# A list-scheduled attention + MoE kernel: one q/k load per head, a first head in halves, warm-up transposes, and a scheduler that leaves spare time behind DMAs

## The chip, the cores and the metric

The kernel runs on one NeuronCore of a Trainium2 chip. TensorE (PE in the profile; its weight loads are PEld) does the matrix products, VectorE (DVE), ScalarE (ACT) and GpSimd (POOL) do the elementwise work, and SyncE (SP) issues the DMAs. Each engine works through its own list of instructions in order; semaphores tie the lists together. The metric is the device time of one launch in microseconds (us): the median of three runs of the kernel before is 790.98 us (788.99 to 792.19).

## The reference

Inputs are float32. Attention has 2 batches, 8 heads, 768 positions and head size 64; a query sees only keys whose 6-bit hash (the signs of a projection) equals its own. Two MLP stages follow on 1536 tokens.

```python
q_bits = (np.einsum('bhsd,dk->bhsk', q, proj) > 0)      # k_bits likewise, 6 bits -> bucket
mask = q_bucket[:, :, :, None] == k_bucket[:, :, None, :]
scores = np.where(mask, scale * np.matmul(q, k.transpose(0, 1, 3, 2)), -1e9)
attn = softmax(scores)                                   # denominator + 1e-9
x = np.matmul(attn, v)            # -> [1536, 512]
g = s * relu(x @ w_in)**2 + b     # w_in [512, 2048]
x = g @ w_out                     # w_out [2048, 512]
h = ((x @ w1) * (x @ w2)) @ w3    # w1, w2 [512, 1024], w3 [1024, 1024]
out = h @ moe2_w_out              # [1024, 512]
```

## The kernel before

Precision comes from splitting: a float32 operand is written as a high and a low float32r part, and one product becomes three matmuls (high·high, low·high, high·low).

**Attention.** There are 16 heads (`heads`), each cut into 3 units of 256 queries (`units`), 48 in all. `load(n)` brings q and k of a head, transposed, into one tile `t` of 128 partitions (q in the lower 64, k in the upper 64) with two DMAs, and v into `tv`. `prep(n)` splits `t` into q1 (high part, `split_h`) and k2 (low part, `split_l`), has TensorE project them on `proj` (`bits`, two halves of 384 columns), turns the signs into plus and minus values (`mask`, VectorE) and moves 64-partition pieces into the four operand tiles q1, q2, k1, k2 (`move`: kh_lo, kh_up, qh, ql, mq, mk). For the first head the moves are copies of 768 columns on ScalarE, VectorE or GpSimd; for the others they are DMAs between on-chip tiles. v is split likewise into `vv` (`vh`, `vl`). `unit(m)` then runs, per 128 queries, the score product (`sc`, 4 matmuls), its row maximum (`negm`), two small factors (`gate`, `bias`) and the exponential on ScalarE (`p`); then the transposes of p (`t`), their split (`pt`) and the product with v (`o`).

**MLP.** `layer1` runs the first MLP for each batch: 32 weight pieces `raw_...` of 512 KB are loaded and converted in six steps (`convert`, `piece`; conv0 to conv5, the first on VectorE, the last on GpSimd or VectorE), saved to DRAM for the second batch (`save_`) and loaded again (`again`). Its products are `h` and `x` (twelve matmuls for a tile), summed into `acc`. `layer2` first folds w3 and the last weight matrix into one (`fold`, tile `psw`: eight steps j of four tiles, for two halves), then computes `a`, `b`, their product `ab` and the output `y`.

**What sets the order.** Nothing is written in its final order. Every operation is handed to `Plan.op` with its engine, an assumed duration, a rank, what it reads and writes, and other engines it may run on instead. `Plan.emit` works out a due time for each operation from the ends backwards (factor table `SLACK`, offsets `AT`), adds a fixed offset by name (`SHIFT`) and then plays a list schedule: whichever engine is free takes the ready operation of lowest rank, with a penalty for waiting (`LOSS`), and an operation is held ready at `free + TAIL + LATE + LAG_TO` after its producer. `LATE` is an extra delay of some DMAs, by name. The tables hold numbers from a search. All loads and DMA moves are issued by SP, in the order of the list.

```python
end = free[e] + self.TAIL[e] + self.late(o)
...
x["ready"][f] = max(x["ready"][f], free[e] if e == f == "pe" else early + self.LAG_TO[f])
```

Of the kernel before, what the change touches and what calls it, by code (L numbers as in the profile page):

```python
# [1033 lines left out]
```

## Time and profile before

| | us |
|---|---|
| median of 3 runs (lowest, highest) | 790.98 (788.99, 792.19) |
| the profiled execution | 791.12 |
| its span, first to last instruction | 789.0 |
| TensorE busy | 756.0 (96%) |
| VectorE busy | 509.1 (65%) |
| ScalarE busy | 404.3 (51%) |
| GpSimd busy | 333.4 (42%) |

Times are counted from the first instruction of the span. TensorE's busy share is near the whole, so the time is its work plus the time it stands idle. TensorE runs at one of two clocks, 1.2 or 2.4 GHz; a granted clock of 1.00 in the windows is the higher, 0.50 the lower one. A wait is put down to the engine and line that ended last before it.

### The profile page before, as it was taken

How to read it: one execution, taken by the hardware profiler on the slowest of the kernel's cores; microseconds unless marked ns; L12 is line 12 of the kernel's file. 1: busy time of each engine (PE TensorE's matmuls, PEld its weight loads, DVE VectorE, ACT ScalarE, POOL GpSimd, SP SyncE). 2: the span in 40 equal slices, each digit the busy share in tenths (PEclk: the TensorE clock that was granted, in tenths of full speed). 3: DMA queues.
4: the chain of work that ended last, by engine and by line, in shares of the span. 5: the costliest groups of instructions: out<-in, count | busy, mean ns of one | idle time of the engine just before them, and what ended most of it. 6: DMA issues, size and time to landing. Idle time of an engine off the chain costs nothing.

```text
span 789.0 us, 12252 instructions
## 1 busy us (share of the span) xinstructions
PE 756.0 (96%) x4464; PEld 712.3 (90%) x4464; DVE 509.1 (65%) x1008; ACT 404.3 (51%) x769; POOL 333.4 (42%) x358
## 2 busy tenths in 40 slices
PE   5999989899999999999999999999999999999997
PEld 4888878799999998999998999889999999999995
DVE  4899998999999989888767664756786010110110
ACT  4888889676576677577453522533554111111111
POOL 2676877674565475554322232223336021121221
PEclk9999999999999999999999999999999999999999
DMA  7445465666575764763348788554421000001001
GB/s 213 121 104 139 104 171 142 189 183 182 182 215 153 228 169 148 218 216 108 107 160 288 257 289 312 187 199 145 166 104 54 1 1 9 32 1 41 1 27 53
DMA packets 36172, 110.83 MB, mean 140 GB/s; under 512 B 5136, under 2 KB 7312, under 8 KB 36112
## 3 DMA queue, kind: packets, MB, share of 16 engines
q1 hardware_dynamic: 36112, 110.06, 45.2%
q8 instruction: 35, 0.57, 0.3%
q14 instruction: 25, 0.20, 0.1%
HBM read 68.22 MB, written 24.12 MB: 117 GB/s over the span
## 4 chain that ended last, share of the span: by engine, by line
PE 70%; DVE 13%; DMA 5%; ACT 5%; issue 3%; POOL 2%; SPq 0%; ACTq 0%; POOLq 0%; DVEq 0%
PE x L721 14%; PE h L721 11%; PE b L721 8%; PE a L721 8%; PE y L972 8%; PE sc L493 5%; PE t L540 5%; DVE negm L503 3%; PE psw L933 3%; PE o L546 3%; PE o L547 3%; DVE pt L582 2%; DMA raw_wo<-in_wo 2%; ACT p L526 2%; DMA raw_w<-in_w3T 2%
## 5 line engine op out<-in xcount | busy, mean ns | idle before, releaser
L721 PE MATMUL x<-g,w_wo 128*128 128x384 f32 x768 | 152.9, 342 | 1.3 <-DVE pt L582 0.7
L721 PE MATMUL h<-x,w_wi 128*128 128x384 f32 x768 | 152.1, 341 | 1.9 <-DVE acc L815 1.7
L721 PEld LDWEIGHTS x<-g,w_wo 128*128 128x128 f32 x768 | 133.4, 189 | 4.7 <-DVE pt L582 1.4
L721 PEld LDWEIGHTS h<-x,w_wi 128*128 128x128 f32 x768 | 132.9, 189 | 4.4 <-DVE acc L815 2.1
L526 ACT ACTIVATE p<-sc,bias,gate 128x768 f32<-128x768 f32 x96 | 95.7, 997 | 30.0 <-DVE bias L518 16.5
L957 DVE SCALAR_TENSOR_TENSOR ab<-b,ab 128x384 f32<-128x384 f32 x32 | 17.8, 558 | 123.9 <-ACT ab L954 123.9
L503 DVE TENSOR_REDUCE negm<-sc 128x1 f32<-128x768 f32 x96 | 90.9, 950 | 9.2 <-PE sc L493 8.4
L963 POOL TENSOR_TENSOR abt<-ab,abt 128x384 fp32r<-128x384 f32 x32 | 33.9, 1061 | 141.5 <-ACT abt L960 141.5
L540 PE MATMUL t<-ident,p 128*128 128x128 f32 x576 | 85.9, 277 | 6.2 <-ACT p L526 2.0
L493 PE MATMUL sc<-k,q 128*128 128x384 f32 x384 | 87.5, 351 | 3.3 <-ACT p L526 2.4
L540 PEld LDWEIGHTS t<-ident,p 128*128 128x128 f32 x576 | 68.6, 142 | 15.2 <-ACT p L526 3.7
L546 PE MATMUL o<-pt,vv 128*128 128x256 f32 x288 | 75.5, 294 | 4.3 <-DVE xf L599 2.8
L336 POOL TENSOR_TENSOR w_w<-raw_w,w_w 128x512 fp32r<-128x512 f32 x31 | 41.7, 1350 | 78.0 <-ACT w_w L334 77.8
L547 PE MATMUL o<-pt,vv 128*128 128x256 f32 x288 | 72.0, 282 | 0.0
L493 PEld LDWEIGHTS sc<-k,q 128*128 128x128 f32 x384 | 66.0, 193 | 6.3 <-ACT p L526 4.0
L721 PE MATMUL a<-x,w_w 128*128 128x384 f32 x384 | 71.1, 334 | 0.0
L721 PE MATMUL b<-x,w_w 128*128 128x384 f32 x384 | 69.7, 335 | 0.0
L582 DVE TENSOR_TENSOR pt<-t,pt 128x512 fp32r<-128x512 f32 x96 | 64.5, 684 | 7.7 <-ACT pt L578 7.2
L721 PEld LDWEIGHTS a<-x,w_w 128*128 128x128 f32 x384 | 67.1, 188 | 0.9
L972 PE MATMUL y<-whl,abt 128*128 128x512 f32 x288 | 67.7, 391 | 0.0
L960 ACT CAST abt<-ab 128x384 fp32r<-128x384 f32 x32 | 16.5, 515 | 99.2 <-PE y L972 96.9
L572 POOL TENSOR_TENSOR pt<-pf,pt 128x512 fp32r<-128x512 f32 x48 | 64.9, 1352 | 5.6 <-ACT pt L568 2.4
(100 smaller groups left out, 1287.4 us busy)
## 6 DMA issues: line engine op xcount, KB each, us to landing
kept_wo<-w_wo SPq DMA_DIRECT2D x24, 512.0 KB, 6.2
w_wo<-kept_wo SPq DMA_DIRECT2D x24, 512.0 KB, 6.0
raw_wi<-in_w_in SPq DMA_DIRECT2D x16, 512.0 KB, 5.2
kept_wi<-w_wi SPq DMA_DIRECT2D x16, 512.0 KB, 3.6
raw_wo<-in_w_out SPq DMA_DIRECT2D x16, 512.0 KB, 5.0
raw_w<-in_w SPq DMA_DIRECT2D x16, 512.0 KB, 3.7
w_wi<-kept_wi SPq DMA_DIRECT2D x16, 512.0 KB, 5.7
raw_w<-in_w3T SPq DMA_DIRECT2D x16, 512.0 KB, 4.4
```

Source lines behind the costliest of these rows:

```text
L336: lambda: nc.gpsimd.tensor_tensor(hl()[:, 1], w, r32(hl()[:, 0]), ALU.subtract),
L493: nc.tensor.matmul(sc()[:, i, :HALF], x[:, t], y[:, i * HALF : (i + 1) * HALF], start=st, stop=not st)
L503: lambda j=j, sc=sc: nc.vector.tensor_reduce(negm()[:, j : j + 1], sc()[:, :, :HALF], AX.XY, ALU.max, negate=True),
L526: lambda j=j, k=k, sc=sc: nc.scalar.activation(ps[j](), sc()[:, :, :HALF], AF.Exp, bias=bias()[:, j : j + 1], scale=gate()[:, j : j + 1], ...
L540: nc.tensor.transpose(tp()[:, e, j * P : (j + 1) * P], flat[:, c * P : (c + 1) * P], ident)
L546: nc.tensor.matmul(o()[:, :U], w, pt()[:, 0, e], start=(c == 0), stop=False)
L547: nc.tensor.matmul(o()[:, :U], w, pt()[:, 1, e], start=False, stop=(c == NC - 1))
L572: lambda pf=pf, pt=pt: nc.gpsimd.tensor_tensor(pt()[:, 1], pf(), r32(pt()[:, 0]), ALU.subtract),
L582: lambda tp=tp, pt=pt: nc.vector.tensor_tensor(pt()[:, 1], tp(), r32(pt()[:, 0]), ALU.subtract),
L721: nc.tensor.matmul(ps()[:, :n], x, y, start=(i == 0 and e == 0), stop=(i == len(terms) - 1 and e == 2))
L963: lambda: nc.gpsimd.tensor_tensor(abt()[:, 1], ab()[:, :TG], r32(abt()[:, 0]), ALU.subtract),
L972: nc.tensor.matmul(y(), abt()[:, p, c], wt()[:, q], start=(i == 0 and e == 0), stop=(i == DF2 // P - 1 and e == 2))
```

## The change

- q and k of a head lie in one input array `qkT`, and a head's tile `t` is one DMA of 128 partitions; the first head's is two, one for each half of the columns.
- The first head's preparation moves to a function of its own, `begin`: every copy is cut in two halves of 384 columns and may run on ScalarE, VectorE or GpSimd; the low part is a subtraction on VectorE; each half waits only for its own half. The first unit's scores wait for the first half of the query operands alone.
- 24 transposes of the identity matrix into an otherwise unused PSUM tile (`warm_up`) stand first on TensorE.
- The scheduler has a table `SPARE`: what a DMA of those names produces counts as ready on the four engines 0.4 to 1.5 us later than before.
- `SLACK`, `AT`, `SHIFT`, `HOLD`, `AHEAD` and `LOSS` hold new numbers, so the order changes in the whole program.

```diff
-SLACK = dict(dma=0.3391, pe=0.5535, dve=0.5716, act=0.4427, pool=0.4279)
+SLACK = dict(dma=0.3487, pe=0.5375, dve=0.5494, act=0.3954, pool=0.4112)
...
-    AHEAD, LOSS = dict(dma=1.714, pe=0.058, dve=0.072, act=0.268, pool=0.156), 39.709
+    AHEAD, LOSS = dict(dma=1.718, pe=0.064, dve=0.089, act=0.249, pool=0.143), 48.706
...
+    SPARE = dict(raw_=1.5, again_=1.5, load_=1.5, kh_=0.5, ql=0.5, qh=0.5, mk=0.4, mq=0.4)
...
+                spare = self.spare(o)
...
-                        x["ready"][f] = max(x["ready"][f], free[e] if e == f == "pe" else early + self.LAG_TO[f])
+                        x["ready"][f] = max(x["ready"][f], free[e] if e == f == "pe" else early + self.LAG_TO[f] + (spare if f != "dma" else 0.0))
...
+        def warm_up():
+            for _ in range(24):
+                nc.tensor.transpose(tw()[:, :P], ident, ident)
+
+        plan.op("warm", "pe", 2.6, -1000, warm_up, [], [(tw, 0)])
...
-            def both():
-                nc.sync.dma_start(t()[0:64], qT[b, h])
-                nc.sync.dma_start(t()[64:128], kT[b, h])
-
-            plan.op(f"load_qk{ph}", "dma", 1.3, LATER, both, (), [(t, 0)])
+            if n == 0:
+                for i in range(2):
+                    c = halves[i]
+                    plan.op(
+                        "load_qk_0", "dma", 0.65, i - 900, lambda c=c: nc.sync.dma_start(t()[:, c], qkT[b, h, :, c]), (), [(t, i)]
+                    )
+            else:
+                plan.op(f"load_qk{ph}", "dma", 0.9, LATER, lambda: nc.sync.dma_start(t(), qkT[b, h]), (), [(t, 0)])
...
+            def ways(key, out, in_, reads, writes):
+                plan.op(
+                    key, "act", 0.4, -500, lambda: nc.scalar.copy(out(), in_()), reads, writes,
+                    (
+                        ("dve", 0.27, lambda: nc.vector.tensor_copy(out(), in_())),
+                        ("pool", 0.42, lambda: nc.gpsimd.tensor_scalar(out(), in_(), 1.0, 1.0, ALU.mult, ALU.mult)),
+                    ),
+                )
...
+            for i in range(2):
+                c = halves[i]
+                last = lambda x, p: [(x, p, 0)] if i else []
+                ways(f"split_h_0{i}", lambda c=c: q1()[:, c], lambda c=c: t()[:, c], [(t, i)], [(q1, 0, i)])
+                plan.op(
+                    f"split_l_0{i}", "dve", 0.47, -500,
+                    lambda c=c: nc.vector.tensor_tensor(k2()[:, c], t()[:, c], r32(q1()[:, c]), ALU.subtract),
+                    [(t, i), (q1, 0, i)], [(k2, 0, i)],
+                )
+                mask(n, i, mm, [(q1, 0, i), (k2, 0, i)])
...
+            if m == 0:
+                need = [(k1, 0), (k1, 1), (k2, 1), (q1, 1, 0), (q2, 0, 0), (q2, 1, 0)]
```

How the instructions stand at three places, before and after. The first is the start of the DMA list on SP and of GpSimd's list: `t` is a head's q and k, `raw_wi` the first MLP's weights, `tv` a head's v, `k_1` the second head's low part. SP before:

```order
L359 DMA pj<-in_projp 128x128
L387 DMA t_169<-in_qT 64x768
L388 DMA t_169<-in_kT 64x768
L387 DMA t_172<-in_qT 64x768
L388 DMA t_172<-in_kT 64x768
L372 DMA s_bc<-in_sv 128x1
L679 DMA raw_wi_0_0_179<-in_w_in 128x1024
L679 DMA raw_wi_0_1_183<-in_w_in 128x1024
L679 DMA raw_wi_0_2_192<-in_w_in 128x1024
```

The same start of SP's list now:

```order
L375 DMA pj<-in_projp 128x128
L416 DMA t_194<-in_qkT 128x384 x2
L743 DMA raw_wi_0_0_197<-in_w_in 128x1024
L743 DMA raw_wi_0_1_199<-in_w_in 128x1024
L743 DMA raw_wi_0_2_201<-in_w_in 128x1024
L419 DMA t_210<-in_qkT 128x768
L420 DMA tv_219<-in_vl 128x384
```

Head 1's load (t_172 before, t_210 now) stood ahead of the three weight loads and stands behind them; its two DMAs are one. GpSimd's first pieces of work after the identity matrix, before:

```order
L418 TENSOR_TENSOR k_0_187<-t_169,q_0_181 128x768
L418 TENSOR_TENSOR k_1_203<-t_172,q_1_194 128x768
L412 TENSOR_SCALAR vv_261<-tv_240 128x6x64
L418 TENSOR_TENSOR vv_261<-tv_240,vv_261 128x6x64
L566 TENSOR_SCALAR pt_1_317<-pf_1_281 128x512
```

GpSimd's first pieces now (q_0 and k_0 are the first head's operands):

```order
L489 TENSOR_SCALAR q_0_213<-q_0_206 64x384 x2
L489 TENSOR_SCALAR q_0_206<-k_0_217 64x384
L441 TENSOR_SCALAR vv_261<-tv_219 128x6x64
L447 TENSOR_TENSOR k_1_263<-t_210,q_1_250 128x768
L630 TENSOR_SCALAR pt_1_336<-pf_1_304 128x512
L636 TENSOR_TENSOR pt_1_336<-pf_1_304,pt_1_336 128x512
```

Both low parts stood ahead of head 0's v (`vv`). Now the copy of v, whose load is issued behind head 1's, stands ahead of head 1's low part `k_1_263`, and the first head's low part has gone to VectorE. On ScalarE head 1's high part still stands ahead of the first exponential.

The second place is VectorE's list where the second batch starts its first MLP (`acc` is the sum that frees a PSUM tile of TensorE, `raw_wo` a weight piece of the last matrix, whose first step is L326, now L342). VectorE before:

```order
L326 TENSOR_SCALAR raw_wo_0_1_1_5734<-raw_wo_0_1_1_5734 128x512
L327 SCALAR_TENSOR_TENSOR raw_wo_0_1_1_5734<-raw_wo_0_1_1_5734 128x512
L333 SCALAR_TENSOR_TENSOR raw_wo_0_1_1_5734<-raw_wo_0_1_1_5734 128x512
L815 COPY acc_5831<-x_3_0_5786 128x384
L326 TENSOR_SCALAR raw_wo_0_2_0_5791<-raw_wo_0_2_0_5791 128x512
L815 COPY acc_5831<-x_3_1_5793 128x384
L327 SCALAR_TENSOR_TENSOR raw_wo_0_2_0_5791<-raw_wo_0_2_0_5791 128x512
L333 SCALAR_TENSOR_TENSOR raw_wo_0_2_0_5791<-raw_wo_0_2_0_5791 128x512
L815 COPY acc_5831<-x_3_2_5802 128x384
```

VectorE at the same place now:

```order
L342 TENSOR_SCALAR raw_wo_0_1_1_5782<-raw_wo_0_1_1_5782 128x512
L879 COPY acc_5836<-x_3_0_5787 128x384
L349 SCALAR_TENSOR_TENSOR raw_wo_0_1_0_5752<-raw_wo_0_1_0_5752 128x512
L879 COPY acc_5836<-x_3_1_5808 128x384
L343 SCALAR_TENSOR_TENSOR raw_wo_0_1_1_5782<-raw_wo_0_1_1_5782 128x512
L349 SCALAR_TENSOR_TENSOR raw_wo_0_1_1_5782<-raw_wo_0_1_1_5782 128x512
L879 COPY acc_5836<-x_3_2_5816 128x384
L879 COPY acc_5836<-x_3_3_5853 128x384
L861 SCALAR_TENSOR_TENSOR rl_2_0_5883<-h_2_0_5842,sw,rl_2_0_5883 128x384
L870 SCALAR_TENSOR_TENSOR g_2_0_5903<-rl_2_0_5883,b_bc,g_2_0_5903 128x384
L342 TENSOR_SCALAR raw_wo_0_2_0_5871<-raw_wo_0_2_0_5871 128x512
```

The first step on piece 0_2_0 stood between the copies of x_3_0 and x_3_1; it now stands behind all four copies, and behind two more operations. Of piece 0_1_1 all three steps stood ahead of the copy of x_3_0; now only the first does, and the others follow the copy of x_3_1.

The third place is TensorE's list at the last steps of the fold (`psw`; w_w_1_4 to w_w_1_7 are converted pieces of w3, `x` the first MLP's second product). TensorE before:

```order
L933 MATMUL psw_0_6480<-w_wo_1_3_0_6404,w_w_1_6_6724 128x512 x3
L933 MATMUL psw_1_6486<-w_wo_1_3_0_6404,w_w_1_6_6724 128x512 x3
L933 MATMUL psw_2_6490<-w_wo_1_3_0_6404,w_w_1_6_6724 128x512 x3
L933 MATMUL psw_3_6495<-w_wo_1_3_0_6404,w_w_1_6_6724 128x512 x3
L721 MATMUL x_3_1_6762<-g_3_0_6528,w_wo_2_0_6252 128x384 x3
L721 MATMUL x_3_1_6762<-g_3_1_6550,w_wo_2_1_6292 128x384 x3
L721 MATMUL x_3_0_6736<-g_3_2_6690,w_wo_2_2_6301 128x384 x3
L721 MATMUL x_2_3_6683<-g_2_3_6521,w_wo_2_3_6333 128x384 x3
L933 MATMUL psw_0_6480<-w_wo_1_3_1_6429,w_w_1_7_6760 128x512 x3
```

TensorE at the fold's steps 4 to 6 now:

```order
L997 MATMUL psw_0_6766<-w_wo_1_2_0_6341,w_w_1_4_6742 128x512 x3
L997 MATMUL psw_1_6777<-w_wo_1_2_0_6341,w_w_1_4_6742 128x512 x3
L997 MATMUL psw_2_6580<-w_wo_1_2_0_6341,w_w_1_4_6742 128x512 x3
L997 MATMUL psw_3_6791<-w_wo_1_2_0_6341,w_w_1_4_6742 128x512 x3
L997 MATMUL psw_0_6766<-w_wo_1_2_1_6378,w_w_1_5_6815 128x512 x3
L997 MATMUL psw_1_6777<-w_wo_1_2_1_6378,w_w_1_5_6815 128x512 x3
L997 MATMUL psw_2_6580<-w_wo_1_2_1_6378,w_w_1_5_6815 128x512 x3
L997 MATMUL psw_3_6791<-w_wo_1_2_1_6378,w_w_1_5_6815 128x512 x3
L997 MATMUL psw_0_6766<-w_wo_1_3_0_6418,w_w_1_6_6842 128x512 x3
L997 MATMUL psw_1_6777<-w_wo_1_3_0_6418,w_w_1_6_6842 128x512 x3
L997 MATMUL psw_2_6580<-w_wo_1_3_0_6418,w_w_1_6_6842 128x512 x3
L997 MATMUL psw_3_6791<-w_wo_1_3_0_6418,w_w_1_6_6842 128x512 x3
```

A step of 12 fold matmuls was followed by 12 of `x` before the next step; now 72 fold matmuls stand in a row, of which the last 36 are shown, and the last step's 12 come three matmuls later.

Further counts over the whole lists: the last conversion step (conv5) stands 3 times on VectorE before and 23 times after, with as many fewer on GpSimd; SP issues 17 loads of q and k instead of 32; ScalarE has 4 fewer casts of whole heads, GpSimd 3 more.

## Rows read from the trace of the kernel before

**Rows 1.** The page: busy time by engine, and the chain of waits by engine.

```profile
PE 756.0 (96%) x4464; PEld 712.3 (90%) x4464; DVE 509.1 (65%) x1008; ACT 404.3 (51%) x769; POOL 333.4 (42%) x358
...
PE 70%; DVE 13%; DMA 5%; ACT 5%; issue 3%; POOL 2%; SPq 0%; ACTq 0%; POOLq 0%; DVEq 0%
```

**Rows 2.** Windows by stage: width, then busy (instructions) of PE, PEld, DVE, ACT, POOL, clock, DMA.

```profile
0.00:24.00 24.00, 13.14 (x47) 11.16 (x48) 11.91 (x34) 12.52 (x20) 7.71 (x12) 0.93 0.71 199
...
40.00:175.00 135.00, 124.48 (x861) 114.44 (x860) 126.49 (x278) 109.38 (x217) 97.84 (x119) 1.00 0.55 144
...
424.00:450.00 26.00, 24.07 (x128) 23.38 (x127) 15.02 (x27) 8.86 (x16) 6.61 (x6) 0.93 0.90 316
...
450.00:600.00 150.00, 148.48 (x785) 138.45 (x784) 101.65 (x169) 64.91 (x113) 50.03 (x42) 1.00 0.55 191
...
782.00:789.00 7.00, 1.92 (x9) 1.26 (x7) 0.69 (x1) 1.17 (x2) 0.00 (x0) 1.00 0.29 112
```

**Rows 3.** Timeline of the first 18 us: start, duration, engine, line, work [idle before <-releaser].

```profile
1.77 0.58 SPq L388 DMA_DIRECT2D t<-in_kT  x1
...
4.30 1.38 SPq L679 DMA_DIRECT2D raw_wi<-in_w_in  x3
...
5.30 0.83 ACT L411 CAST q<-t 128x768 fp32r<-128x768 f32 x1 [3.08 <-DMA t<-in_kT]
...
8.78 1.82 POOL L418 TENSOR_TENSOR k<-t,q 128x768 fp32r<-128x768 f32 x1 [0.76 <-ACT q L411]
...
11.14 2.77 PE L493 MATMUL sc<-k,q 128*128 128x384 f32 x8
...
12.66 0.96 DVE L503 TENSOR_REDUCE negm<-sc 128x1 f32<-128x768 f32 x1 [0.54 <-PE sc L493]
...
15.76 0.99 ACT L526 ACTIVATE p<-sc,bias,gate 128x768 f32<-128x768 f32 x1 [4.46 <-DVE gate L511]
...
16.90 0.97 PE L493 MATMUL sc<-k,q 128*128 128x384 f32 x4 [2.16 <-ACT p L526]
```

**Rows 4.** The tile raw_wi in the first 40 us: the three weight loads' landing.

```profile
DMA to landing us min/median/max: 5.4/6.4/8.3
```

**Rows 5.** Windows of the head, columns as in rows 2.

```profile
0.00:4.00 4.00, 0.00 (x0) 0.00 (x0) 1.03 (x12) 1.49 (x2) 0.69 (x6) 1.00 0.43 116
...
8.00:12.00 4.00, 3.63 (x10) 3.13 (x11) 2.90 (x5) 2.36 (x3) 1.85 (x2) 1.00 0.96 343
...
15.00:17.00 2.00, 0.10 (x1) 0.10 (x1) 0.94 (x4) 1.24 (x3) 0.00 (x0) 1.00 0.83 187
...
18.00:21.00 3.00, 3.00 (x13) 2.90 (x14) 2.15 (x4) 1.61 (x3) 2.57 (x4) 0.50 0.60 137
```

**Rows 6.** Timeline: eight transposes in that last window.

```profile
19.85 1.73 PE L540 MATMUL t<-ident,p 128*128 128x128 f32 x8
```

**Rows 7.** Timeline around 432 us, VectorE and TensorE.

```profile
432.53 0.43 DVE L326 TENSOR_SCALAR raw_wo<-raw_wo 128x512 int32<-128x512 uint32 x1 [2.28 <-DMA raw_wo<-in_wo]
...
433.47 0.79 PE L721 MATMUL h<-x,w_wi 128*128 128x384 f32 x3 [1.74 <-DVE acc L815]
```

**Rows 8.** A window behind it, columns as in rows 2.

```profile
434.00:438.00 4.00, 4.00 (x16) 4.00 (x15) 1.31 (x4) 1.33 (x2) 1.30 (x1) 0.57 0.92 338
```

**Rows 9.** Chain of waits, order of time: start, duration, work (the last four folds).

```profile
526.02 2.80 PE psw L933 x11
...
541.71 2.76 PE psw L933 x12
```

**Rows 10.** Groups by line and shape: busy us, mean ns | idle before, releasers.

```profile
L336 POOL TENSOR_TENSOR w_w<-raw_w,w_w 128x512 fp32r<-128x512 f32 x31 | 41.7, 1350 | 78.0 <-ACT w_w L334 77.8
...
L412 POOL TENSOR_SCALAR vv<-tv 128x384 fp32r<-128x384 f32 x5 | 2.6, 517 | 8.0 <-DMA tv<-in_vl 7.7 <-PE o L547 0.3
...
L337 DVE TENSOR_TENSOR w_w<-raw_w,w_w 128x512 fp32r<-128x512 f32 x1 | 0.7, 696 | 0.0
...
L420 DVE TENSOR_TENSOR vv<-tv,vv 128x384 fp32r<-128x384 f32 x3 | 1.9, 632 | 0.7 <-ACT vv L411 0.7
```

More of the change, by code (lines that the diff above doesn't have):

```diff
@@ L182, in late, with spare @@
         return next((v for k, v in self.LATE.items() if o["engine"] == "dma" and o["key"].startswith(k)), 0.0)
+    def spare(self, o):
+        return next((v for k, v in self.SPARE.items() if o["engine"] == "dma" and o["key"].startswith(k)), 0.0)
     def early(self, o):
@@ L368, in lsh_attention_moe @@
         )
+        tw = plan.tile(ps_t, 3, [P, 512], F32, "t", "warm")
+        def warm_up():
+            for _ in range(24):
+                nc.tensor.transpose(tw()[:, :P], ident, ident)
+        plan.op("warm", "pe", 2.6, -1000, warm_up, [], [(tw, 0)])
         for x, t, src in (("s", s_bc, sv), ("b", b_bc, bv)):
@@ L378, in phase @@
             return "s" if n == 0 else heads[n][0]
+        halves = [slice(i * HALF, (i + 1) * HALF) for i in range(2)]
         def load(n):
@@ L440, in prep @@
-            copy(f"split_h{ph}", (0.73, 0.8), q1, t, [(t, 0)], [(q1, 0)])
-            rest(f"split_l{ph}", 1.8, k2, t, q1, [(t, 0), (q1, 0)], [(k2, 0)])
-            mm = plan.tile(raw_p, 1, [P, S], F32R, "mm", f"mm_{n}")
-            for i in range(2):
-                mask(n, i, mm)
-            bits = [(mm, 0), (mm, 1)]
-            move(f"kh_lo{ph}", k1, lo, q1, up, [(q1, 0)], [(k1, 0)])
-            move(f"kh_up{ph}", k1, up, q1, up, [(q1, 0)], [(k1, 1)])
-            move(f"qh{ph}", q2, up, q1, lo, [(q1, 0)], [(q2, 0)])
@@ L449, in prep @@
-            move(f"ql{ph}", q1, up, k2, lo, [(k2, 0), (k1, 0), (k1, 1), ("bits", n, 0), ("bits", n, 1)], [(q1, 1)])
-            move(f"mq{ph}", q2, lo, mm, lo, bits, [(q2, 1)])
-            move(f"mk{ph}", k2, lo, mm, up, bits + [(q1, 1)], [(k2, 1)])
+                plan.op(key, "dma", 0.65, LATER, lambda: nc.sync.dma_start(r32(out()[a]), r32(in_()[z])), reads, writes)
+            if first:
+                begin(n)
+            else:
+                copy(f"split_h{ph}", (0.73, 0.8), q1, t, [(t, 0)], [(q1, 0)])
+                rest(f"split_l{ph}", 1.8, k2, t, q1, [(t, 0), (q1, 0)], [(k2, 0)])
+                mm = plan.tile(raw_p, 1, [P, S], F32R, "mm", f"mm_{n}")
+                for i in range(2):
+                    mask(n, i, mm)
+                bits = [(mm, 0), (mm, 1)]
+                move(f"kh_lo{ph}", k1, lo, q1, up, [(q1, 0)], [(k1, 0)])
+                move(f"kh_up{ph}", k1, up, q1, up, [(q1, 0)], [(k1, 1)])
+                move(f"qh{ph}", q2, up, q1, lo, [(q1, 0)], [(q2, 0)])
+                move(f"ql{ph}", q1, up, k2, lo, [(k2, 0), (k1, 0), (k1, 1), ("bits", n, 0), ("bits", n, 1)], [(q1, 1)])
+                move(f"mq{ph}", q2, lo, mm, lo, bits, [(q2, 1)])
+                move(f"mk{ph}", k2, lo, mm, up, bits + [(q1, 1)], [(k2, 1)])
@@ L457, in prep, with begin, move, mask @@
             )
-        def mask(n, i, mm):
+        def begin(n):
+            t, _ = raws[n]
+            q1, q2, k1, k2, _ = ops[n]
+            lo, up = slice(0, 64), slice(64, 128)
+            mm = plan.tile(raw_p, 1, [P, S], F32R, "mm", f"mm_{n}")
+            def ways(key, out, in_, reads, writes):
[6 more added lines that the diff above has]
+                )
+            def move(key, i, x, a, y, z, reads, writes):
+                c = halves[i]
+                ways(f"{key}_0{i}", lambda: x()[a, c], lambda: r32(y()[z, c]), reads, writes)
+            for i in range(2):
+                c = halves[i]
+                last = lambda x, p: [(x, p, 0)] if i else []
[6 more added lines that the diff above has]
+                mask(n, i, mm, [(q1, 0, i), (k2, 0, i)])
+                move("kh_lo", i, k1, lo, q1, up, [(q1, 0, i)] + last(k1, 0), [(k1, 0, i)] + ([(k1, 0), (q1, 0), (k2, 0)] if i else []))
+                move("kh_up", i, k1, up, q1, up, [(q1, 0, i)] + last(k1, 1), [(k1, 1, i)] + ([(k1, 1)] if i else []))
+                move("qh", i, q2, up, q1, lo, [(q1, 0, i)], [(q2, 0, i)] + ([(q2, 0)] if i else []))
+                move(
+                    "ql", i, q1, up, k2, lo, [(k2, 0, i), (k1, 0, i), (k1, 1, i), ("bits", n, i)],
+                    [(q1, 1, i)] + ([(q1, 1)] if i else []),
+                )
+                move("mq", i, q2, lo, mm, lo, [(mm, i)], [(q2, 1, i)] + ([(q2, 1)] if i else []))
+                move("mk", i, k2, lo, mm, up, [(mm, i), (q1, 1, i)] + last(k2, 1), [(k2, 1, i)] + ([(k2, 1)] if i else []))
+        def mask(n, i, mm, need=None):
             q1, _, _, k2, _ = ops[n]
```

35 lines of the change are left out of this document (10 added, 25 removed), and 132 rows, old and new, of tables (AT, SHIFT).

## The prediction

> **What bounds the kernel now.** I read the page first. TensorE is busy 756.0 us [rows 1] of a span of 789.0 us, so 33.0 us of idle time is all that an order can win, apart from time at the lower clock. Then the windows by stage [rows 2] say where those 33 us lie: 10.9 us in the first 24 us, 10.5 us from 40 to 175 us, 1.9 us from 424 to 450, 1.5 us from 450 to 600, 5.1 us in the last 7 us; the remaining 3.1 us are spread over the other stretches. From 40 to 175 us VectorE is busy 126.5 of 135 us, so there TensorE waits on VectorE's work, which this change hardly touches. The end is a copy and a DMA, which stay. Two places are left in which the edits can act: the head, and the dip at 432 us.
>
> In the head I read the timeline [rows 3]. The load of k is issued at 1.77 us and ScalarE's split starts at 5.30 us. GpSimd's low part follows, then projections, masks and moves, and the first row maximum stands at 12.66 us. The first exponential starts at 15.76 us and the third group of scores, which has to wait for it, at 16.90 us. From 15 to 17 us TensorE does 0.1 us of work, and the window 18 to 21 us then shows the granted clock at 0.50, the 1.2 GHz level [rows 5]: 1.5 us of full-speed work is lost in it.
>
> At 432 us the timeline [rows 7] shows one in-order stop. VectorE's first step on a weight piece waits 2.28 us for its DMA. The copy of `acc` that frees a PSUM tile stands behind it, and TensorE's next `h` has waited 1.74 us when it starts at 433.47 us. In the 4 us from 434 on the granted clock is 0.57 on the mean [rows 8], which loses 4 x 0.43 = 1.72 us. So this stop costs 1.74 + 1.72 = 3.46 us.
>
> **The change part by part.** The profiled execution took 791.12 us, 2.12 us more than its span and 0.14 us above the median of 790.98 us; I sum against 791.12 us and take the sum as the forecast of the median.
>
> First head in halves. It has the same bytes in the same two issues, so I let the second half land when k does now, about 5.2 us. ScalarE and VectorE cast the halves by then or 0.4 us later. VectorE subtracts each half; the nearest row is the 128x384 subtraction at 632 ns [rows 10], so both low parts are there at about 6.9 us, where GpSimd's whole one starts when the cast ends, at 6.13 us, and takes 1.82 us, to 8.0 us [rows 3]. Two masks and two half moves follow, all on VectorE; at about 0.5 us each, somewhat less than that subtraction, the second operand is there at 8.8 us and the first row maximum can start near 9.3 us instead of 12.66 us: 3.4 us earlier (2.5 to 4 by the unknown casts). From the first maximum to the first exponential 3.1 us pass now [rows 3], with a mask of the second head and a gap among them; I take 2.2 us without these, so the exponential could start at 11.5 us.
>
> The second head, however, loses its place. Its load stood ahead of the three 512 KB weight loads and now stands behind them. On ScalarE its cast stands ahead of the first exponential, and on TensorE its projection stands ahead of the third group of scores. Behind the cast on ScalarE wait both first exponentials, and behind the projection wait all later scores and transposes. When does it land? The last weight load is issued at 5.3 us and lands 8.3 us later, the longest of the three, at 13.6 us [rows 3, 4]. Now the three are issued 1.9 us earlier, since three small issues no longer stand ahead, so the last would land at 11.7 us, and 393 KB more at the 343 GB/s of 8 to 12 us [rows 5] take 1.15 us: 12.85 us. By bytes alone it could be 9.7 us: 2.42 MB stand ahead or are its own, 0.46 MB are moved by 4 us at 116 GB/s [rows 5], and 1.96 MB at 343 GB/s take 5.7 us. If the weights land no earlier than now, it is 14.8 us. I take 12.5 us, near the end that rests on a landing, not on bytes.
>
> From there: head 0's v lands 0.57 us later (197 KB at 343 GB/s), GpSimd casts it in 0.52 us [rows 10], makes the low part in 1.82 us [rows 3], and one projection matmul at the pitch that eight scores show (2.77 us for 8, [rows 3]) takes 0.33 us: 3.24 us in all. The third group of scores so starts at 15.74 us instead of 16.90 us. **Head: 1.2 us gained**; with 9.7 us it is 4.0 us gained, with 14.8 us 1.1 us lost. The 3.4 us that the halves win are thus mostly waited away behind the weights. Everything after is bound by VectorE or TensorE, both of which start earlier by the same amount, so I carry it to the end undiminished.
>
> Warm-up. The 24 transposes start within the first 2 us on an engine that has nothing to do before the first cast ends at 6.13 us. Eight transposes at the lower clock take 1.73 us [rows 6], so 24 end by 7.2 us at the latest, up to 1.0 us after the first half's operands are there. The wait for the second head hides that; without this cover it costs 1.0 us. They lift the clock for the first scores only: after those TensorE waits for the second head from about 10 to 15.7 us. The rows show that after 2 us with hardly any work, from 15 to 17 us, the clock fell to 0.50 [rows 5]. I therefore leave the 1.5 us of clock loss in the sum. The Trainium skill's page TensorE: Matmul & The Clock Gate (HAM oscillation — how this bites in real kernels) says the same against this edit: a long gap on TensorE throws the clock back, whatever was warmed before. By that rule the sum keeps the 1.5 us; were the clock to hold, it would lose them. The trace agrees with the rule at 17 us and at 434 us.
>
> One load for q and k. SP issues 15 loads fewer, of about 0.6 us each, but SP's queue has 0% of the chain of waits [rows 1]; the cover is that later heads are loaded long before their use. Worth nothing; without that cover 0.6 us a head. The Trainium skill's page DMA: Bandwidth & Descriptors (Rules for kernel authors) says that transfers to disjoint halves of the partitions serialize and one of 128 partitions should be used. By it each pair would shorten a little; the rows of the head show 343 GB/s without it, so I add nothing.
>
> Spare time and new ranks. At the 432 us stop the changed order puts the first step on the next piece behind all four copies of `acc`, so that exact stop goes. What is late next there is piece 0_1_1, whose first step stands ahead of the copy of x_3_0. It is issued when VectorE's new last step on piece 0_0_1 has freed its buffer, and some nine operations of about 0.6 us and three `x` tiles lie between, so it is nearly landed when asked for. **3.46 us gained**, between 0 (a like stop in its place) and 3.46.
>
> Conversions on VectorE: 20 more last steps at 696 ns are 13.9 us, where GpSimd needs 1350 ns [rows 10]. Most are after 424 us, where VectorE is busy 117 of 176 us [rows 2]; that slack hides them. Exposed, each would cost at most its 0.7 us. Elsewhere the counts of work between equal score groups differ by a few operations, so I put 0 for the 40 to 175 us stretch, with 2 us either way.
>
> Sum: 791.12 - 1.2 - 3.46 = 786.5 us.
>
> **The rivals.**
>
> The stop comes back. If piece 0_1_1 or another load is some 2 us late with the copies behind it, as at 432 us, the 3.46 us are paid again and only the head is won: 791.12 - 1.2 = 789.9 us. For it: SP holds the same pieces in nearly the same sequence. Against: the first step stands behind more copies.
>
> Slower: folds in a row. TensorE has 72 fold matmuls in a row, where other products lay between. In the trace the last four steps start 15.69 us / 3 = 5.23 us apart, one takes 2.76 us [rows 9]. If the pieces of w3 are converted only at the old pace when TensorE reaches step 4, it waits 2.47 us at each of three steps, 7.4 us: 791.12 - 1.2 - 3.46 + 7.4 = 793.9 us, slower than before. It decides as soon as three pieces come more than 2.76 us apart and the lead of the 36 matmuls ahead is used up. For it: VectorE converts pieces 1_5 to 1_7 just there. Against: those last steps are faster on VectorE, and 36 matmuls are 8.3 us of lead.
>
> Faster than I think: the second head lands at 9.7 us, by bytes, and the gap on TensorE is short enough that the clock holds: 791.12 - 4.0 - 1.5 - 3.46 = 782.2 us. For it: 96% DMA share from 8 to 12 us, so loads really stream. Against: the 8.3 us landing, far behind the bytes.
>
> **How the numbers follow.** The forecast has 0.45, the stop's return 0.25, the folds 0.17, the fast head 0.13. The forecast's own range is 784.0 to 789.0 us (the 40 to 175 us stretch, and the landing). For 8 in 10 I take 781.5 to 793.5 us: it holds the fast head nearly and half of the folds' case. What can be told from no change is 0.5%, 3.95 us: faster is below 787.0 us, slower above 794.9 us. Faster: 0.27 of the forecast's case, all 0.13 of the fast head, 0.02 of the rest, 0.42. Slower: 0.08 of the folds and 0.04 of mishaps beyond the cases, 0.12. The same: 0.46.
>
> **What would show it.** The first row maximum near 9.3 us and the first exponential only after the second head's cast, near 13.3 us, show the halves and the lost place. The third group of scores near 15.7 us shows the head's gain; at 13 us the landing was early, after 16.9 us the head has lost. A window at 0.50 clock between 14 and 20 us shows that the warm-up did not last. No clock window below 1.00 between 420 and 450 us, and no wait of `h` on `acc` above 1 us, show the stop gone. Waits of `psw` of more than 1 us in a row of folds would show the slower rival. I am wrong if the idle time of the 40 to 175 us stretch moves by more than 2 us, since I have put it at nothing.

## The result and the profile after

The changed kernel takes 783.16 us (median of 4 runs, 782.39 to 784.66); the kernel before takes 790.05 us in runs on the same chip (4 runs, 788.99 to 792.19). The ratio is 0.9906, 95% interval 0.9878 to 0.9935. The forecast of 786.5 us had the direction and the two places; the gain is 6.9 us where it had 4.6. The time lies 0.8 us below the forecast's own range of 784.0 to 789.0 us and inside the wider one of 781.5 to 793.5 us. The profiled execution took 784.66 us, 6.46 us less than that of before; its span is 6.1 us shorter.

The page of the kernel after, the two lines that answer to [rows 1]:

```profile
PE 757.7 (97%) x4488; PEld 712.8 (91%) x4488; DVE 522.8 (67%) x1031; ACT 402.8 (51%) x772; POOL 312.9 (40%) x340
...
PE 72%; DVE 18%; ACT 4%; DMA 3%; issue 1%; POOL 1%; SPq 0%; ACTq 0%; POOLq 0%; DVEq 0%
```

VectorE does 13.7 us more and DMA fell from 5% to 3% of the chain. The windows by stage, which answer to [rows 2] (width; busy time and instructions of PE, PEld, DVE, ACT, POOL; clock, DMA share, GB/s):

```profile
0.00:24.00 24.00, 18.29 (x90) 16.02 (x91) 16.88 (x42) 13.60 (x26) 8.41 (x15) 0.86 0.67 199
...
40.00:175.00 135.00, 125.34 (x862) 114.76 (x861) 127.64 (x279) 109.58 (x219) 94.97 (x117) 1.00 0.53 147
...
424.00:450.00 26.00, 26.00 (x152) 25.95 (x151) 18.42 (x34) 11.32 (x21) 4.77 (x4) 1.00 0.80 272
450.00:600.00 150.00, 149.50 (x794) 140.02 (x793) 106.27 (x181) 64.98 (x112) 32.18 (x25) 1.00 0.57 200
...
776.00:783.00 7.00, 1.71 (x8) 1.09 (x6) 0.69 (x1) 1.17 (x2) 0.00 (x0) 0.79 0.29 112
```

From 424 to 450 us TensorE neither waits nor slows down; before it was idle for 26 - 24.07 = 1.93 us there and lost 0.07 x 26 = 1.82 us at the lower clock. From 450 to 600 us its idle time fell from 1.52 to 0.50 us. The last 7 us are nearly as they were: 5.3 us idle where it was 5.1. For the first 24 us the timeline says more; these rows answer to [rows 3] and [rows 7] (start, duration, engine, line, work [idle before <-releaser]):

```profile
3.84 0.51 ACT L486 CAST q<-t 128x384 fp32r<-128x384 f32 x1 [1.63 <-DMA t<-in_qkT]
...
9.04 1.15 PE L553 MATMUL sc<-k,q 128*128 128x384 f32 x5 [0.67 <-DVE k L488]
...
9.52 1.82 DVE L567 TENSOR_REDUCE negm<-sc 128x1 f32<-128x768 f32 x2 [0.54 <-PE sc L553]
...
11.45 0.83 ACT L440 CAST q<-t 128x768 fp32r<-128x768 f32 x1 [2.38 <-DMA t<-in_qkT]
...
12.53 0.99 ACT L590 ACTIVATE p<-sc,bias,gate 128x768 f32<-128x768 f32 x1 [0.25 <-DVE gate L575]
...
14.93 1.48 PE L553 MATMUL sc<-k,q 128*128 128x384 f32 x4
...
428.34 0.43 DVE L342 TENSOR_SCALAR raw_wo<-raw_wo 128x512 int32<-128x512 uint32 x1 [0.52 <-DMA raw_wo<-in_wo]
429.11 0.56 DVE L879 COPY acc<-x 128x384 f32<-128x384 f32 x1 [0.34 <-PE x L785]
...
529.49 16.54 PE L997 MATMUL psw<-w_wo,w_w 128*128 128x512 f32 x72
```

```profile
118.24 1.25 PE L553 MATMUL sc<-k,q 128*128 128x384 f32 x4
...
120.29 1.21 PE L493 MATMUL sc<-k,q 128*128 128x384 f32 x4
```

The first row maximum stands 3.14 us earlier than before, but ScalarE then waits 2.38 us for the second head's load; the third group of scores stands at 14.93 us, 1.97 us earlier. The gain lasts: the same group of scores starts at 118.24 us after and at 120.29 us before (second fence). At 428 us a weight piece is still late, by 0.52 us, but no copy misses its time behind it. The 72 folds in a row run in 16.54 us without a wait. The clock in the head, answering to [rows 5]:

```profile
10.00:12.00 2.00, 0.18 (x2) 0.00 (x0) 1.50 (x3) 0.55 (x1) 0.00 (x0) 1.00 0.72 257
12.00:14.00 2.00, 1.01 (x2) 0.50 (x2) 1.81 (x5) 1.75 (x4) 1.90 (x2) 0.52 0.29 71
14.00:16.00 2.00, 1.55 (x5) 1.56 (x6) 1.48 (x2) 0.59 (x2) 0.39 (x1) 0.50 0.91 220
16.00:18.00 2.00, 2.00 (x9) 1.90 (x8) 1.32 (x3) 0.70 (x2) 0.03 (x1) 0.50 0.92 295
18.00:21.00 3.00, 2.99 (x18) 2.70 (x17) 2.38 (x5) 2.19 (x5) 1.87 (x2) 0.85 0.29 64
```

After 2 us with 0.18 us of work the 1.2 GHz level is back until almost 19 us (from 18 to 19 us the clock reads 0.54): the warm-up does not survive the wait for the second head. One run of the kernel with the first head loaded whole, 828.56 us at a mean clock of 0.85 where its other three show 0.995 to 0.997, is left out below.

### The profile page after: what moved, and what is told of

The parts are those of the page before. It is cut to its first block, busy times and chain, and to the rows that moved or that the text cites. A ratio compares the mean times of both kernels' runs of the same rounds, so it can differ in the third digit from the quotient of the medians.

```text
span 782.9 us, 12258 instructions
## 1 busy us (share of the span) xinstructions
PE 757.7 (97%) x4488; PEld 712.8 (91%) x4488; DVE 522.8 (67%) x1031; ACT 402.8 (51%) x772; POOL 312.9 (40%) x340
## 4 chain that ended last, share of the span: by engine, by line
PE 72%; DVE 18%; ACT 4%; DMA 3%; issue 1%; POOL 1%; SPq 0%; ACTq 0%; POOLq 0%; DVEq 0%
PE x L785 13%; PE h L785 13%; PE a L785 9%; PE b L785 9%; PE y L1036 8%; PE psw L997 6%; PE t L604 5%; PE sc L553 4%; DVE negm L567 4%; DVE pt L646 3%; PE o L610 2%; PE o L611 2%; DVE g L870 2%; ACT p L590 1%; PE bits L525 1%
## 5 line engine op out<-in xcount | busy, mean ns | idle before, releaser
L785 PE MATMUL x<-g,w_wo 128*128 128x384 f32 x768 | 146.8, 339 | 1.0 <-DVE rl L861 0.7
L604 PE MATMUL t<-ident,p 128*128 128x128 f32 x576 | 84.2, 276 | 5.3 <-DVE pt L646 2.2
L604 PEld LDWEIGHTS t<-ident,p 128*128 128x128 f32 x576 | 67.0, 141 | 15.8 <-DVE pt L646 4.1
L642 ACT CAST pt<-t 128x512 fp32r<-128x512 f32 x96 | 54.5, 587 | 25.5 <-PE o L611 14.8
L785 PEld LDWEIGHTS b<-x,w_w 128*128 128x128 f32 x384 | 67.1, 188 | 0.2
```

Of the source, the lines that this page charges most:

```text
L604: nc.tensor.transpose(tp()[:, e, j * P : (j + 1) * P], flat[:, c * P : (c + 1) * P], ident)
L642: lambda tp=tp, pt=pt: nc.scalar.copy(pt()[:, 0], tp()), [(tp, 0)], [(pt, 0)],
L785: nc.tensor.matmul(ps()[:, :n], x, y, start=(i == 0 and e == 0), stop=(i == len(terms) - 1 and e == 2))
```

## Experiments

Three sets of runs on three chips; each kernel is compared by its ratio with the kernel before of the same set (791.72, 791.66 and 793.23 us). The spans of one kernel's executions differ by 3.1 us for the best one (777.1 to 780.2, 4 runs) and by 6.9 us for the kernel before in one set (786.0 to 792.9, 13 runs), so a smaller difference in the last column counts only where the timeline shows its place.

| kernel | us, median | ratio to before [95%] | profiled span |
|---|---|---|---|
| after, from above | 783.16 | 0.9906 [0.9878, 0.9935] | 782.9 |
| one warm-up transpose | 783.51 | 0.9887 [0.9861, 0.9914] | 781.6 |
| second head ahead of weights | 781.84 | 0.9872 [0.9844, 0.9901] | 779.8 |
| same, scale too | 781.09 | 0.9860 [0.9834, 0.9887] | 778.7 |
| before, one step exchanged | 791.01 | 0.9996 [0.9974, 1.0019] | 788.3 |
| before, six steps moved | 793.17 | 1.0015 [1.0000, 1.0030] | 791.6 |
| scale too, early half | 780.23 | 0.9858 [0.9836, 0.9881] | 777.1 |
| no spare time, weights | 797.94 | 1.0077 [1.0052, 1.0101] | 798.4 |
| no spare time, moves | 797.44 | 1.0069 [1.0047, 1.0091] | 797.4 |
| first head whole | 782.50 (3 runs) | 0.9887 [0.9851, 0.9923] | 780.3 |
| early half, first head whole | 781.22 | 0.9858 [0.9834, 0.9882] | 779.4 |
| early half, one warm-up | 781.92 | 0.9868 [0.9846, 0.9890] | 780.4 |
| two loads a head | 785.87 | 0.9918 [0.9894, 0.9942] | 784.8 |

**One warm-up transpose** in the kernel after.

```diff
-            for _ in range(24):
+            for _ in range(1):
```

> The changed kernel with 1 warm-up transpose instead of 24; every instruction else stands where it stood. My theory (the head is set by the landing of the second head's load behind the weights, and the warm-up buys nothing behind the first scores): the first scores run at the lower clock and the first row maximum comes up to 1 us later than 9.52 us, but ScalarE's cast of the second head still starts near 11.45 us and the third group of scores near 14.9 us, so the span stays within 0.5 us of 782.9 us. Rival (the warm-up earns the head's gain): the third group of scores goes back towards 16.9 us and the span grows by 1 to 2 us.

The ratio is within the interval of the kernel after. The timeline of this kernel:

```profile
9.15 1.97 PE L553 MATMUL sc<-k,q 128*128 128x384 f32 x5 [0.42 <-DVE k L488]
...
11.84 0.83 ACT L440 CAST q<-t 128x768 fp32r<-128x768 f32 x1 [2.65 <-DMA t<-in_qkT]
...
15.26 1.48 PE L553 MATMUL sc<-k,q 128*128 128x384 f32 x4
```

Five scores take 1.97 us (1.15 us in the kernel after), yet the second head's cast comes after them either way and the third scores start only 0.33 us later. The cast itself starts 0.39 us later, behind its DMA. Warming up is worth at most 0.33 us here, and nothing that the time shows.

**The second head's load ahead of the weights.** Only the order on SP is changed: its q and k and the first head's v stand ahead of the three 512 KB loads; in a second kernel the scale `s_bc` too.

```diff
+        for o in (tv, load):            # second kernel: (scale, tv, load)
+            issued.remove(o)
+            issued.insert(raw, o)       # raw: the first weight load
```

> The changed kernel with the second head's load and the first head's v ahead of the three weight loads on SP; nothing else moves. My theory: the load lands before 9 us, ScalarE's cast follows the last copy at 9.1 us, GpSimd's low part ends near 12 us instead of 14.4. VectorE's small factor sw still waits for its load (12.16 us) ahead of the first bias, so the first exponential stays near 12.5 us, and the third group of scores starts near 13.6 us instead of 14.93: 1.3 us off the span, 781.6 us. Rival (the weights are needed early and pay it back, or the gain is swallowed by VectorE from 40 us on): the third scores come earlier, but the span stays at 782.9 us or grows.

> As the run before, with the load of the scalar s ahead of the weights too. My theory: sw no longer waits, the first exponential starts near 11.6 us, the third group of scores near 12.7 us: 2.2 us off the span of the changed kernel, 780.7 us, and up to 1.5 us more if the shorter gap on TensorE keeps the clock at the higher level, 779.2 us. Rival as in the run before: 782.9 us.

In the trace both are faster than the kernel after, by 3.1 and 4.2 us of span; the ratios point the same way, with intervals that overlap its own. In the first kernel the third scores start at 13.58 us, as expected, but the clock still falls, to 0.68 from 14 to 18 us. The second kernel's timeline, and two of its windows:

```profile
8.50 0.83 ACT L447 CAST q<-t 128x768 fp32r<-128x768 f32 x1
...
12.78 0.97 PE L560 MATMUL sc<-k,q 128*128 128x384 f32 x4 [1.06 <-ACT p L597]
```

```profile
18.00:21.00 3.00, 3.00 (x25) 2.76 (x25) 2.60 (x7) 1.53 (x5) 0.69 (x1) 1.00 0.57 124
21.00:24.00 3.00, 1.60 (x10) 1.07 (x9) 0.69 (x1) 2.98 (x7) 2.92 (x3) 1.00 0.64 169
```

The cast waits for no DMA, the third scores come 2.15 us earlier than in the kernel after, the clock stays at 1.00, and no wait of TensorE from 5 to 24 us is longer than 1.1 us. So the places of these small loads, the second head's above all, were what ate the halves' gain. Part is lost again from 21 to 24 us, where the second head's scores wait for its masks, which SP moves only after the low part.

**The second head's other half early.** That stall is taken away by putting the second half's projection and mask right behind the first half's.

```diff
+        for late, early in ((bits00, bits10), (mask00, mask10)):   # the second head's
+            issued.remove(late)
+            issued.insert(issued.index(early) + 1, late)
```

> The kernel with the second head's load, its v and the scale ahead of the weights, with the second half of the second head's projection and its mask put right behind the first half on TensorE and VectorE. There TensorE did 1.60 us of work from 21 to 24 us and waited for the chain projection, on-chip move of the low part, on-chip move of the masks. Theory (that chain is what ate the head's last gain): the chain starts some 2.5 us earlier, TensorE works at least 2.8 of the 3 us from 21 to 24, and the span falls from 778.7 to about 777.3 us. Rival (the mask ahead of the third row maximum delays the exponentials by 0.7 us, or VectorE sets the pace from there on): the time is the same within 0.5 us or above.

The windows of this kernel:

```profile
14.00:18.00 4.00, 3.42 (x23) 2.89 (x23) 3.54 (x8) 3.16 (x6) 1.89 (x2) 1.00 0.97 249
18.00:21.00 3.00, 2.99 (x24) 2.72 (x24) 2.58 (x7) 2.76 (x7) 1.99 (x3) 1.00 0.47 104
21.00:24.00 3.00, 3.00 (x21) 2.65 (x21) 2.54 (x6) 2.86 (x7) 2.37 (x2) 1.00 0.83 210
```

The stall is gone: TensorE works all of the 3 us from 21 us on, and the span is 777.1 us, where 777.3 was expected. This kernel has the shortest span and median: 0.9858 of before against 0.9906 for the change as it was made; the two intervals just overlap. The ratio does not tell it from the kernel with the scale moved (0.9860), so what this last step is worth in every execution is open.

**The stop at 432 us by hand**, in the kernel before: the stalled first step exchanged with the copy behind it, then all six steps of that piece moved behind the fourth copy.

```diff
+        issued.remove(conv)
+        issued.insert(issued.index(copy) + 1, conv)    # first kernel: step 0 behind x_3_1
...
+        issued[at:at] = conv                           # second: steps 0 to 5 behind x_3_3
```

> The kernel before with two neighbours on VectorE exchanged: the first step on weight piece 0_2_0 behind the copy of x_3_1 instead of ahead of it. My theory (at 432 us TensorE waits for that copy, which waits behind the step for its DMA): TensorE's wait of 1.74 us there goes, the clock stays up or falls for less than 3 us, and the span falls by 1.7 to 3.5 us, to 785.5 to 787.3 us. Rival (TensorE waits for something else there, such as the next copy or the weights, or the time is lost again later): the wait moves by a few us and the span stays at 789.0 us.

> The kernel before, with all six conversion steps of weight piece 0_2_0 moved behind the fourth copy of acc (x_3_3), not only the first step. Theory (the stop at 432 us is a stalled step in front of the copies, and 3.46 us is its price): neither the wait of 1.74 us at 432 us nor the one of 1.44 us that the exchange of one step left at 436 us is there, the granted clock stays 1.00 from 424 to 450 us, and the span falls from 789.0 to 785.5 us (up to 786.5 if a part is lost again later). Rival (the piece is wanted at that pace anyway): the six steps end later, the products that read the piece wait instead, and the span is 788 us or more.

TensorE's timeline in the first kernel and in the second, each with a window:

```profile
432.04 0.68 PE L725 MATMUL h<-x,w_wi 128*128 128x384 f32 x3
...
436.24 3.93 PE L725 MATMUL h<-x,w_wi 128*128 128x384 f32 x21 [1.44 <-DVE acc L819]
...
434.00:438.00 4.00, 2.56 (x15) 2.24 (x14) 2.40 (x5) 1.31 (x2) 1.31 (x1) 1.00 0.98 370
```

```profile
435.06 4.84 PE L727 MATMUL h<-x,w_wi 128*128 128x384 f32 x27
441.71 3.94 PE L727 MATMUL h<-x,w_wi 128*128 128x384 f32 x21 [1.80 <-DVE rl L803]
447.33 4.96 PE L727 MATMUL h<-x,w_wi 128*128 128x384 f32 x27 [1.68 <-DVE rl L803]
...
442.00:446.00 4.00, 3.65 (x21) 3.33 (x20) 1.36 (x3) 1.81 (x4) 1.21 (x1) 1.00 0.93 232
```

In both the wait of 1.74 us at 433 us and the low clock are gone, so the cause was named rightly. The time does not fall for it. One step moved still stands, with its own wait of 1.34 us for the DMA, in front of the other copies, and so does the third step, which waits 0.78 us for ScalarE: 1.44 us. Six steps moved pile up behind the copies and delay the products `rl` that free the tiles of `h`: 1.80 and 1.68 us. The theory that 3.46 us come back when the stalled steps go behind the copies fell: moved by hand in these two ways, they did not. From 424 to 450 us the second kernel is idle for 3.48 us, about what was lost there before. The first loses only 1.59 us there, yet its interval leaves no more than 0.26%, 2.1 us, of gain. The clock loss is no fixed price of such a wait: behind 1.74 us the clock fell to 0.57 [rows 8], behind 1.80 us it reads 1.00 here, and 21 products take 3.94 us as in the first kernel (3.93).

**Spare time taken away**, in the kernel after: behind weight loads, and in a second kernel behind the on-chip moves; each order is computed anew.

```diff
-    SPARE = dict(raw_=1.5, again_=1.5, load_=1.5, kh_=0.5, ql=0.5, qh=0.5, mk=0.4, mq=0.4)
+    SPARE = dict(load_=1.5, kh_=0.5, ql=0.5, qh=0.5, mk=0.4, mq=0.4)     # weights
+    SPARE = dict(raw_=1.5, again_=1.5, load_=1.5)                        # moves
```

> The kernel after, with the spare time taken away behind the weight loads only (raw and again; the entries for the heads' loads and moves stay, as do all other numbers), so the whole order is computed anew. Theory (spare time behind weight loads keeps their first conversion step from standing stalled ahead of copies): VectorE or ScalarE waits of more than 1 us for a raw or again DMA come back with a wait of TensorE behind them, and the time is 2 to 6 us above that of after. Rival (the searched ranks alone did it, spare time is idle): no such wait of TensorE, time within 1 us of after.

> The kernel after, with the spare time taken away behind the on-chip moves only (kh, qh, ql, mk, mq; loads keep theirs), the order computed anew with the same other numbers: as far from a searched order as the one without spare time behind weights. Theory (only weight loads come late by enough to matter): 0 to 1.5 us above after, by scattered waits between 24 and 424 us, none of more than 1 us on a weight load. Rival (any order that was not searched loses the same): as much above after as the kernel without spare time behind the weights, within 1 us.

Both lose about 1.7% to the kernel after, far more than expected and equally much, as the rival had it: the tables were searched for one order, and two orders that were not searched cost this. The total therefore says nothing of spare time. The waits do; the timeline of the first kernel, then of the second:

```profile
326.53 0.43 DVE L342 TENSOR_SCALAR raw_wo<-raw_wo 128x512 int32<-128x512 uint32 x1 [2.65 <-DMA raw_wo<-in_w_out]
...
328.68 1.32 PE L785 MATMUL x<-g,w_wo 128*128 128x384 f32 x6 [3.10 <-DVE acc L881]
```

```profile
144.01 1.31 PE L553 MATMUL sc<-k,q 128*128 128x384 f32 x6 [1.45 <-DMA k<-mm]
...
163.11 3.19 DVE L870 SCALAR_TENSOR_TENSOR g<-rl,b_bc,g 128x384 fp32r<-128x384 f32 x2
...
166.96 1.97 PE L604 MATMUL t<-ident,p 128*128 128x128 f32 x8 [3.64 <-DVE pt L646]
```

Without spare time behind weights a stop of the kind of 432 us stands at 326 us, and TensorE waits 3.10 us behind it. Without spare time behind moves TensorE waits for a move, and VectorE waits at most 1.1 us for a weight load. That wait is the smaller part: idle time from 40 to 175 us is 16.7 us, where the kernel after has 9.7, and the longest wait, 3.64 us, is for VectorE, which stands behind two steps on `g` that take 3.19 us (see the last section). How much of the 3.75 us is owed to spare time and how much to the new ranks stays open, since each was only searched with the other.

**The first head in one load**, in the kernel after and in the best kernel.

```diff
-  "load_qk_0", ..., lambda c=c: nc.sync.dma_start(t()[:, c], qkT[b, h, :, c])
+  "load_qk_0", ..., lambda i=i: i or nc.sync.dma_start(t(), qkT[b, h])
```

> The kernel after, with the first head's q and k loaded in one piece of 768 columns instead of two halves; everything else stands in the same order. Theory (the halves' gain is waited away behind the second head's load): the first cast starts at about 4.5 instead of 3.84 us and the first row maximum 0.4 to 0.8 us after 9.52 us, but the second head's cast still starts between 11.0 and 11.5 us and the third scores at 14.5 to 15.0 us (14.93 in after): span 782.9 within 0.5 us. Rival (the halves earn the head's gain): third scores 0.5 us or more later than in after, span 783.4 us or more.

> The same undoing of the halves in the kernel with the second head ahead of the weights and its two half projections together (span 777.1 us, first row maximum near 9.5 us, third scores at 13.00 us). There nothing waits for the second head's load, so by the theory that the halves only count where that load is early, the third scores come 0.4 to 0.8 us later and the span is 777.5 to 777.9 us. Rival (the halves never count, GpSimd's and VectorE's work of the second head sets the pace): third scores within 0.2 us of 13.00, span 777.1 within 0.3.

The timeline of the first of the two:

```profile
4.49 0.51 ACT L486 CAST q<-t 128x384 fp32r<-128x384 f32 x1 [2.28 <-DMA t<-in_qkT]
...
10.41 0.83 ACT L440 CAST q<-t 128x768 fp32r<-128x768 f32 x1 [0.89 <-DMA t<-in_qkT]
...
13.67 0.86 PE L553 MATMUL sc<-k,q 128*128 128x384 f32 x4
```

Neither account had this. The first cast is 0.65 us later, but with one issue fewer everything behind it on SP goes 0.46 us earlier, the second head's cast starts 1.04 us earlier and the third scores 1.26 us earlier; the ratio, 0.9887, stays within the interval of the kernel after. In the best kernel, where no load is waited for, the third scores start at 13.23 instead of 13.00 us, less than expected; the span is 2.3 us longer and the ratio the same. By these single traces splitting the load is worth 0.23 us in that head, and costs 1.26 us in the other; what both kernels keep, the copies in halves and the low part on VectorE, goes with the earlier first maximum (9.97 us here against 12.66). The two were not tested apart.

**One warm-up transpose in the best kernel.**

> One warm-up transpose instead of 24 in the kernel with the second head ahead of the weights and its two half projections together. There the granted clock is 1.00 in the whole head with 24. Theory (the warm-up is worth something only where no long gap follows): the projections and first scores run at the lower clock, the third scores start 0.3 to 0.8 us after 13.00 us, and the span is 777.4 to 778.0 us. Rival (the head's pace is set by VectorE, ScalarE and GpSimd, the clock does not matter there): third scores within 0.2 us, span 777.1 within 0.3.

Its timeline, and a window of it:

```profile
13.68 1.65 PE L564 MATMUL sc<-k,q 128*128 128x384 f32 x4 [0.26 <-ACT p L601]
...
18.39 0.95 PE L564 MATMUL sc<-k,q 128*128 128x384 f32 x4
```

```profile
14.00:16.00 2.00, 2.00 (x9) 1.90 (x9) 1.03 (x2) 0.60 (x2) 0.00 (x0) 1.00 1.01 290
```

The third scores start 0.68 us later, within what was expected, and four of them take 1.65 us instead of 0.96; the span is 3.3 us longer, more than expected, while the ratio, 0.9868 against 0.9858, does not tell them apart. By the traces the warm-up earns something, 0.68 us, only where no long wait follows.

**Two loads for each later head**, in the kernel after.

```diff
-  lambda: nc.sync.dma_start(t(), qkT[b, h])
+  nc.sync.dma_start(t()[0:64], qkT[b, h, 0:64])
+  nc.sync.dma_start(t()[64:128], qkT[b, h, 64:128])
```

> The kernel after, with q and k of every head but the first loaded by two DMAs of 64 partitions, as before: 15 more issues of SP, the order of all else unchanged. Theory (the one load is worth nothing, SP is not on the path): the second head's cast within 0.5 us of 11.45 us, span 782.9 within 0.7 us. Rival (transfers to half the partitions are slower or an issue more delays what stands behind): second head's cast 0.6 us or more later and the third scores with it, span 783.6 us or more.

A window and the timeline of this kernel, and for its second half load the time to landing; then that time for the kernel after's loads of line 419, the longest of which is the second head's:

```profile
8.00:10.00 2.00, 1.14 (x5) 0.92 (x6) 1.33 (x4) 0.61 (x2) 0.00 (x0) 1.00 1.03 269
...
14.39 0.83 ACT L444 CAST q<-t 128x768 fp32r<-128x768 f32 x1 [5.09 <-DMA t<-in_qkT]
...
17.75 1.48 PE L557 MATMUL sc<-k,q 128*128 128x384 f32 x4
```

```profile
DMA to landing us min/median/max: 10.2/10.2/10.2
```

```profile
DMA to landing us min/median/max: 3.3/6.2/7.9
```

The theory fell, at least in the trace: the pair lands at 4.12 + 10.2 = 14.3 us, one load at 3.52 + 7.9 = 11.4 us, and the third scores are 2.82 us later. In this trace what stands ahead of the pair is slowed too: from 8 to 10 us the DMA engines are as busy as in the kernel after (1.03 and 1.01) but move 269 GB/s instead of 383, and the last weight load, issued at the same time in both, lands 10.3 us after its issue instead of 7.4. The ratios, 0.9918 and 0.9906, do not separate the two, so how much of the 2.9 us every execution pays is open.

## Why the prediction came out as it did

**Head: forecast 1.2 us, measured 2.0 us.** The mechanism was right, and the size was off: first maximum at 9.52 us (forecast 9.3), the first exponential behind the second head's cast, the rest waited away. The mis-sized term is the landing of the second head: 11.4 us, where 12.5 was taken. It rested on the last weight load landing 8.3 us after its issue [rows 4], and that time fell to 7.4 us. Fewer and undivided small loads are the likely reason, since the two-load kernel has 10.3 us, but in the change as made they were not tested apart. The chain behind it took 3.48 us, forecast 3.24.

**Warm-up: forecast hidden and not lasting.** Right: the low clock stands from 12 to almost 19 us, and one transpose instead of 24 costs nothing measurable. The prediction counted the low clock from 18 us on only. The eight scores at 11.14 us [rows 3] take 0.35 us each; five take 0.39 us each with one transpose and 0.23 us each with 24. So the lower pace stood earlier too, under a clock that reads 1.00.

**One load: forecast worth nothing.** The reason given, that heads are loaded long before use, does not hold for the second head, which the prediction itself had found late. The Trainium skill's page DMA: Bandwidth & Descriptors (Rules for kernel authors) holds that two transfers to half the partitions each bring nothing over one; the trace of two loads agrees and goes further, with 14.3 against 11.4 us.

**Stop at 432 us: forecast 3.46 us, measured 1.93 + 1.82 = 3.75 us.** Right in place and size. It came with a whole new order; each of the two moves by hand turned it into a new wait.

**Conversions on VectorE: forecast hidden, measured a gain of 1.0 us** from 450 to 600 us. Before, the folds waited 0.9 us, in two waits, for GpSimd's last steps; after, for nothing. That VectorE's steps did it is read from these waits; no run moved the conversions alone. What the prediction had wrong here is the term that it put at nothing: slack hides the cost of these steps on VectorE, but it counted no gain from them. This and the head's 0.8 us are most of what the forecast missed. The terms 2.0 + 3.75 + 1.0 make 6.75 us, and the span is 6.1 us shorter, so 0.65 us was lost elsewhere: idle time rose by 0.82 us from 24 to 40 us, 0.24 us from 175 to 424 us and 0.21 us in the last 7 us. From 40 to 175 us idle time went from 10.52 to 9.66 us, inside the 2 us allowed.

**Rivals.** The stop did not come back, and the folds did not wait; that VectorE's faster last steps kept pace fits, but was not tested alone. Of the fast head the landing came part of the way (11.4 us, between 12.5 and 9.7) and the clock did not hold. It came fully once the three small loads were moved: then the clock holds, third scores start at 12.8 to 13.0 us, and the time is 780.2 to 781.1 us, where that rival had 782.2. The prediction gave "the same", within 0.5%, its highest chance, 0.46; the gain is 0.9%.

## What to carry to other kernels

When an edit makes the first step ready earlier, follow the next input in the DMA queue: what stands ahead of it there decides whether the gain is kept; here three small loads moved past weights that are first multiplied at about 133 us brought the third scores another 2.15 us forward, more than splitting and warming up had (1.97 us). A stalled in-order step was priced rightly here by the wait and the clock behind it, but two moves by hand earned nothing: the work has to go somewhere. Taking a part out of a searched schedule can cost more than the part (1.7% in both cases here), so read such an undoing by its waits, not by its time.
